# Linear attention with a highway layer: q in two-chunk pieces, weights loaded as f32, feed-forward in groups of two chunks, and another order in the fill

## The chip, the cores and the metric

The kernel runs on one core of a Trainium2 chip. A core has five engines that each run their own queue of instructions: TensorE (PE in the profile; its weight loads are PEld), VectorE (DVE), ScalarE (ACT), GpSimd (POOL) and SyncE (SP), which here only issues DMAs. Loads and stores run on 16 DMA engines. Matrix products are written to PSUM, which has eight banks; all else lies in SBUF. The metric is device time in microseconds, the median of ten runs. Lower is better.

## What is computed

Two stages follow one another. The first is a causal linear attention with a decay lam per head, over batch 4, 8 heads, 768 positions and head size 64:

```python
# in blocks; kv_state is 64 x 64 per batch and head
intra = (q_b @ k_b.T * Dmask) @ v_b          # Dmask[i, j] = lam**(i-j) for j <= i, else 0
inter = (q_b * lam_pow) @ kv_state
out_b = intra + inter
kv_state = lam_block * kv_state + (k_b * rev_pow).T @ v_b
```

The second takes the attention's output as x, 3072 tokens of 512 features, and applies a highway layer with two 512 x 512 weights:

```python
H = np.maximum(x @ w_h, 0.0)
T = 1.0 / (1.0 + np.exp(-(x @ w_t + b_t)))
out = T * H + (1.0 - T) * x
```

Inputs and output are f32. The kernel computes the products in bf16, and the last line as x + T * (max(x @ w_h, 0) - x).

## The kernel before

**Tiling.** Positions are cut in chunks of C = 128 tokens, six to a batch, so there are N = 24 chunks over the four batches. All 8 heads of a chunk are worked on together, as NP = 4 pairs of heads. The feed-forward takes G = 4 chunks at a time (512 tokens, GT), as four units, one for each 128 output features.

**Steps of a chunk n.** `cast_k` (L130) makes bf16 of k, and `scale_v` (L135) multiplies v by a power of lam and makes bf16 of it; both are on POOL. `trans_k` transposes k on PE with four transposes into the PSUM tile `tr`, and ACT copies that to `kT` (L166, L168). `scores` (L176) multiplies k by q with eight matmuls on half of the array, and DVE masks the result with a triangle (L179). `inter` (L187) applies the state `s_bd` to q, `intra` (L194) adds the masked scores times v into the same PSUM tile `o_ps`, and DVE scales that by `pow_q` into `xT` (L199). `state` (L208) adds the chunk to the state kept in PSUM, which ACT copies to `s_bd` in two halves (L212). The last chunk of a batch has no `state`, and the first has no `inter`.

**q.** Batch 0 is loaded chunk by chunk in rows of 256 bytes (`load_q0`, L67), cast by `cast_q0` and transposed by `trans_q0` (L146, L147). Batches 1 to 3 are loaded one pair of heads at a time with J = 6 tokens to a partition, in rows of 1536 bytes (`load_q`, L63), cast on POOL (L151), and transposed by `trans_q` in six transposes (L159) with one ACT copy that puts the tokens back in order (L160).

**Feed-forward.** `ffn_h` (L217) forms x @ w_h for one 128-feature slice in four matmuls of 512 columns, and DVE makes max(.,0) - x of it (L220). `ffn_t` (L225) does the same for w_t, with a sigmoid on ACT (L228) and a product on DVE (L231). `ffn_out` (L238) brings one chunk back to token order, adding x and the product with eight matmuls against the identity. ACT copies it to SBUF (L242; DVE for some of the last chunks, L244), and SP stores it (L245).

**PSUM.** Every tag has one buffer: `tr`, `s` (two banks), `o`, `kv`, `h`, `t` and `x` fill the eight banks. The next user of a tile waits for the reader of the last one.

**Order.** The order is written by hand: each engine runs its instructions in the order in which the program emits them. The loop's turn i emits the casts of chunk i+3, then `trans_k(i+2)`, `inter(i)`, `scores(i+1)`, `intra(i)`, `state(i)`, a q transpose, one feed-forward unit with one `ffn_out` between its two halves, and the loads of chunk i+8 (LA = 8). All loads of k, v and q are on SP's queue, and so are the stores. The two weights are loaded on POOL's queue with a cast to bf16 (L271, L272), after chunk 1's casts. The fill before the loop takes chunk 0 to its scores and chunk 1 to its transposes. Units of a group are queued when its last chunk is through `state`.

Of the kernel before, what the change touches and what calls it, by code (L numbers as in the profile page):

```python
# [16 lines left out]
def kernel(  # L17
# [43 lines left out]
    def load_q(b, hp):  # L61
        qf[b, hp] = load.tile([128, 2, J * D], F32, tag="qf", name="qf", bufs=6)
        nc.sync.dma_start(out=qf[b, hp], in_=q[b, 2 * hp:2 * hp + 2].rearrange("e (p j) d -> p e (j d)", j=J))  # L63

    def load_q0(c):
        q0f[c] = load.tile([C, H, D], F32, tag="q0f", name="q0f", bufs=4)
        nc.sync.dma_start(out=q0f[c], in_=q[0, :, c * C:(c + 1) * C, :].rearrange("h p d -> p h d"))  # L67

    def loads(n):
        if n >= N:  # L70
            return
        b, c = divmod(n, NCH)
        load_k(n)
        if b == 0:
            load_q0(c)
        load_v(n)
        if c < NP and b + 1 < B:
            load_q(b + 1, c)
# [40 lines left out]
    pow_q = singles.tile([128, NP, NCH * C], F32)  # L119
    for hp in range(NP):  # L120
        nc.scalar.activation(pow_q[:, hp, 0:C], tq_f[:, 0:C], AF.Exp, scale=ln_hp[:, hp:hp + 1])

    qb, kb, qT, kT, vs, masked, xT, thmx, hmx, kv_ps, o_ps = ({} for _ in range(11))

    def cast_k(n, eng=None):
        b, c = divmod(n, NCH)
        kb[n] = work.tile([C, H, D], BF16, tag="kb", name="kb", bufs=4)
        (eng or nc.gpsimd).tensor_copy(kb[n], kf[n])  # L130

    def scale_v(n):
        b, c = divmod(n, NCH)
        vs[n] = work.tile([C, H, D], BF16, tag="vs", name="vs", bufs=4)
        nc.gpsimd.tensor_tensor(vs[n], in0=vf[n], in1=pow_k[:, :, c, :].to_broadcast([C, H, D]), op=ALU.mult)  # L135

    def cast_q0(c, eng=None):
        qb[c] = work.tile([C, H, D], BF16, tag="q0b", name="q0b")
        (eng or nc.gpsimd).tensor_copy(qb[c], q0f[c])

    def trans_q0(c):
        if 0 not in qT:
            qT[0] = load.tile([128, NP, S], BF16, tag="qT", name="qT0")
        tr = ps.tile([128, NP, C], BF16, tag="tr", name="tr")
        for hp in range(NP):
            nc.tensor.transpose(tr[:, hp, :], qb[c][:, 2 * hp:2 * hp + 2, :], id128)  # L146
        nc.scalar.activation(qT[0][:, :, c * C:(c + 1) * C], tr, AF.Copy)  # L147

    def cast_q(b, hp):
        qb[b, hp] = work.tile([128, J, 2, D], BF16, tag="qb", name="qb")  # L150
        nc.gpsimd.tensor_copy(qb[b, hp].rearrange("p j e d -> p e j d"),  # L151
                              qf[b, hp].rearrange("p e (j d) -> p e j d", j=J))

    def trans_q(b, hp):
        if hp == 0:
            qT[b] = load.tile([128, NP, S], BF16, tag="qT", name=f"qT{b}")
        tr = ps.tile([128, J, 128], BF16, tag="tr", name="tr")
        for j in range(J):
            nc.tensor.transpose(tr[:, j, :], qb[b, hp][:, j], id128)  # L159
        nc.scalar.activation(qT[b][:, hp].rearrange("p (q j) -> p q j", j=J),  # L160
                             tr.rearrange("p j q -> p q j"), AF.Copy)
# [7 lines left out]

    def scores(n):  # L170
        b, c = divmod(n, NCH)
        s_ps = ps.tile([C, 2, NP, C], F32, tag="s", name="s_ps")
        for hp in range(NP):
            for e in range(2):
                r = slice(64 * e, 64 * e + 64)
                nc.tensor.matmul(s_ps[:, e, hp, :], lhsT=kT[n][r, hp, :], rhs=qT[b][r, hp, c * C:(c + 1) * C], start=True, stop=True)  # L176
# [4 lines left out]

    def inter(n):
        b, c = divmod(n, NCH)
        o_ps[n] = ps.tile([128, NP, C], F32, tag="o", name="o_ps")
        if c > 0:
            for hp in range(NP):
                nc.tensor.matmul(o_ps[n][:, hp, :], lhsT=s_bd[n % 2][:, hp, :], rhs=qT[b][:, hp, c * C:(c + 1) * C],  # L187
                                 start=(hp == 0), stop=False, skip_group_check=True)
# [25 lines left out]
    def ffn_h(g, j):  # L214
        h_ps = ps.tile([128, GT], F32, tag="h", name="h_ps")
        for kc in range(KC):
            nc.tensor.matmul(h_ps, lhsT=wh[:, kc, j * 128:(j + 1) * 128], rhs=xT[g][:, kc, :],  # L217
                             start=(kc == 0), stop=(kc == KC - 1))
        hmx[g, j] = work.tile([128, GT], BF16, tag="hmx", name="hmx")
        nc.vector.scalar_tensor_tensor(hmx[g, j], in0=h_ps, scalar=0.0, in1=xT[g][:, j, :], op0=ALU.max, op1=ALU.subtract)  # L220

    def ffn_t(g, j):
        t_ps = ps.tile([128, GT], F32, tag="t", name="t_ps")
        for kc in range(KC):
            nc.tensor.matmul(t_ps, lhsT=wt[:, kc, j * 128:(j + 1) * 128], rhs=xT[g][:, kc, :],  # L225
                             start=(kc == 0), stop=(kc == KC - 1))
        t_sb = work.tile([128, GT], BF16, tag="t_sb", name="t_sb")
        nc.scalar.activation(t_sb, t_ps, AF.Sigmoid, bias=bt_col[:, j:j + 1])  # L228
        if j == 0:
            thmx[g] = work.tile([128, NP, GT], BF16, tag="thmx", name="thmx")  # L230
        nc.vector.tensor_tensor(thmx[g][:, j, :], in0=t_sb, in1=hmx[g, j], op=ALU.mult)  # L231
# [19 lines left out]
    trans_k(0)
    trans_q0(0)
    scores(0)
    id_f = singles.tile([KC, KC], F32)
    nc.vector.tensor_copy(id_f, id128[0:KC, 0:KC])
    bt_ps = ps.tile([128, KC], F32, tag="x", name="bt_ps")
    nc.tensor.transpose(bt_ps, bt_r, id_f)
    bt_col = singles.tile([128, KC], F32)
    nc.vector.tensor_copy(bt_col, bt_ps)
    for n in range(4, LA):  # L260
# [1 line left out]
    cast_k(1)
    cast_q0(1)
    scale_v(1)
    trans_k(1)
    trans_q0(1)
    for hp in range(NP):
        nc.scalar.activation(pow_q[:, hp, C:], tq_f[:, C:], AF.Exp, scale=ln_hp[:, hp:hp + 1])
    wh = singles.tile([128, KC, DM], BF16)
    wt = singles.tile([128, KC, DM], BF16)  # L270
    nc.gpsimd.dma_start(out=wh, in_=moe_w_h.rearrange("(kc p) n -> p kc n", p=128))  # L271
    nc.gpsimd.dma_start(out=wt, in_=moe_w_t.rearrange("(kc p) n -> p kc n", p=128))  # L272
    cast_k(2)
    scale_v(2)
    cast_q0(2)
# [4 lines left out]
    while i < N or units or outs:  # L280
        b, c = divmod(i, NCH)
# [3 lines left out]
        if i + 3 < NCH:  # L285
            cast_q0(i + 3)
        if c < NP and b + 1 < B:
            cast_q(b + 1, c)
# [9 lines left out]
        if i + 2 < NCH:  # L298
            trans_q0(i + 2)
        if 1 <= c <= NP and b + 1 < B:  # L300
            trans_q(b + 1, c - 1)
        unit = units.pop(0) if units else None
        if unit:
            ffn_h(*unit)
        if outs:
            ffn_out(outs.pop(0), "dve" if i >= N and i % 2 else "act")
        if unit:
            ffn_t(*unit)
            if unit[1] == NP - 1:
                outs += range(unit[0] * G, unit[0] * G + G)  # L310
        if i < N and i % G == G - 1:
            units += [(i // G, j) for j in range(NP)]
# [32 lines left out]
```

## Time and profile before

| | |
|---|---|
| median of 10 runs | 138.34 us (137.11 to 139.17) |
| the profiled execution | 137.11 us, of which the span from the first to the last instruction is 135.2 us |
| PE busy | 101.4 us (75% of the span), 1105 instructions |
| DVE busy | 74.1 us (55%) |
| ACT busy | 77.6 us (57%) |
| POOL busy | 54.4 us (40%) |
| DMA | 26.40 MB in 64101 packets, of which 56916 are under 512 bytes |
| SP's and ACT's DMA packets | 77.9% of the 16 engines' span |
| the weights' packets (POOL's queue) | 4.7% |

Busy time is an average over stages that differ. In the slices of the profile each digit is the busy share of one fortieth of the span, in tenths. In the windows, the columns are the stretch in us, its length, then busy time and number of instructions of PE, PEld, DVE, ACT and POOL, then the granted TensorE clock as a share of full speed, the busy share of the DMA engines, and GB/s. A DMA share above 1 means that packets overlap. In the timeline, a line has its start, its length, the engine, the line of the kernel, the operation, what it writes and reads, and in brackets how long the engine had been idle and what ended that. Matmuls overlap in the array, so the length of a row of matmuls goes some 0.17 us beyond the start of the next.

### The profile page before, as it was taken

The page shows a single profiled execution, that of the slowest core. Times are in us where ns is not written, and L with a number is a line of the kernel's source. Part 1 is how long each engine was busy: PE and PEld are TensorE (multiplying, and loading weights), DVE is VectorE, ACT ScalarE, POOL GpSimd, SP SyncE. Part 2 cuts the span into 40 slices and gives each one's busy share as a digit, 9 for nine tenths or more (in the row PEclk, how much of TensorE's full clock was granted, in tenths as well). Part 3 has the DMA queues.
Part 4 walks back from the last instruction along what each step waited for, and adds up shares of the span by engine and source line. Part 5 has one row for each costly group of instructions (what it writes and reads, how often), then busy time and mean ns, then how long its engine had stood idle before and what let it go on. Part 6 is the DMA issues. An engine that isn't in the chain of part 4 may idle for free.

```text
span 135.2 us, 2889 instructions
## 1 busy us (share of the span) xinstructions
PE 101.4 (75%) x1105; PEld 67.1 (50%) x1121; DVE 74.1 (55%) x133; ACT 77.6 (57%) x141; POOL 54.4 (40%) x76
## 2 busy tenths in 40 slices
PE   0134520367674999999999999999999999999440
PEld 0122410345463655667766666766666665555330
DVE  4403230050432559976668878666887778656320
ACT  3752950144436665778885788887666766444310
POOL 5047620185596436767345776733243000000000
PEclk9999999999999599999999999999999999999975
DMA  2999999999999999999999999999222212224262
GB/s 62 257 245 266 235 191 213 231 233 225 184 257 268 259 266 192 219 266 215 229 265 273 260 253 256 267 276 263 87 82 78 78 62 81 94 78 158 82 228 78
DMA packets 64101, 26.40 MB, mean 195 GB/s; under 512 B 56916, under 2 KB 61016, under 8 KB 64088
## 3 DMA queue, kind: packets, MB, share of 16 engines
q1 hardware_dynamic: 62880, 25.17, 77.9%
q0 software_dynamic: 1056, 1.05, 4.7%
q8 instruction: 8, 0.13, 0.4%
q14 instruction: 5, 0.04, 0.1%
q10 hardware_dynamic: 152, 0.01, 0.1%
HBM read 20.98 MB, written 6.29 MB: 202 GB/s over the span
## 4 chain that ended last, share of the span: by engine, by line
PE 68%; SPq 9%; DMA 9%; ACT 6%; issue 3%; POOL 2%; DVE 1%; POOLq 0%; ACTq 0%
PE h_ps L217 16%; PE t_ps L225 15%; PE x_ps L238 9%; DMA kf<-in_k_dram 9%; PE o_ps L194 6%; PE s_ps L176 5%; PE kv_ps L208 5%; PE tr L159 4%; PE tr L166 4%; SPq L59 4%; PE o_ps L187 3%; SPq L63 3%; SPq L67 2%; ACT qT L160 2%; ACT qT L147 1%
## 5 line engine op out<-in xcount | busy, mean ns | idle before, releaser
L179 DVE TENSOR_TENSOR masked<-s_ps,tri 128x512 bf16<-128x512 f32 x48 | 30.8, 682 | 28.8 <-PE s_ps L176 28.8
L135 POOL TENSOR_TENSOR vs<-vf,pow_k 128x512 bf16<-128x512 f32 x24 | 25.4, 1059 | 22.3 <-DMA vf<-in_v_dram 11.0
L217 PE MATMUL h_ps<-xT,wh 128*128 128x512 bf16 x85 | 24.6, 389 | 0.7 <-issue 0.2
L225 PE MATMUL t_ps<-xT,wt 128*128 128x512 bf16 x91 | 24.4, 381 | 0.2
L130 POOL CAST kb<-kf 128x512 bf16<-128x512 f32 x23 | 14.1, 614 | 24.7 <-DMA kf<-in_k_dram 13.1
L166 PE MATMUL tr<-id,kb 128*128 128x128 bf16 x96 | 10.6, 240 | 16.7 <-POOL kb L130 8.9
L228 ACT ACTIVATE t_sb<-t_ps,bt_col 128x512 bf16<-128x512 f32 x24 | 16.5, 687 | 11.3 <-PE t_ps L225 9.8
L231 DVE TENSOR_TENSOR thmx<-t_sb,hmx 128x512 bf16<-128x512 bf16 x24 | 10.3, 429 | 20.0 <-ACT t_sb L228 19.7
L168 ACT ACTIVATE kT<-tr 128x512 bf16<-128x512 bf16 x24 | 14.2, 590 | 12.3 <-PE tr L166 12.3
L212 ACT ACTIVATE s_bd<-kv_ps 64x256 bf16<-64x256 f32 x40 | 15.1, 378 | 10.4 <-PE kv_ps L208 9.6
L166 PEld LDWEIGHTS <-kb 128*128 128x128 bf16 x96 | 7.8, 107 | 21.7 <-POOL kb L130 9.5
L242 ACT ACTIVATE o_sb<-x_ps 128x512 f32<-128x512 f32 x20 | 11.9, 597 | 11.2 <-PE x_ps L238 11.2
L220 DVE SCALAR_TENSOR_TENSOR hmx<-h_ps,xT 128x512 bf16<-128x512 f32 x24 | 16.3, 680 | 1.5 <-PE h_ps L217 1.5
L199 DVE TENSOR_TENSOR xT<-o_ps,pow_q 128x512 bf16<-128x512 f32 x24 | 16.3, 679 | 0.0
L238 PE MATMUL x_ps<-id,xT 128*128 128x128 bf16 x96 | 13.6, 222 | 2.6 <-ACT o_sb L242 1.4
L238 PE MATMUL x_ps<-id,thmx 128*128 128x128 bf16 x96 | 13.9, 223 | 0.4 <-DVE thmx L231 0.4
L238 PEld LDWEIGHTS <-thmx 128*128 128x128 bf16 x96 | 9.5, 99 | 6.2 <-issue 3.1
L217 PEld LDWEIGHTS <-wh 128*128 128x128 bf16 x96 | 8.6, 100 | 7.3 <-issue 0.6
L225 PEld LDWEIGHTS <-wt 128*128 128x128 bf16 x96 | 8.7, 99 | 7.0 <-issue 0.8
L160 ACT ACTIVATE qT<-tr 128x768 bf16<-128x768 bf16 x12 | 9.7, 811 | 2.6 <-PE tr L159 2.4
L176 PE MATMUL s_ps<-qT,kT 64*128 64x128 bf16 x192 | 10.6, 236 | 0.7 <-ACT qT L147 0.7
L194 PE MATMUL o_ps<-masked,vs 128*64 128x128 bf16 x192 | 10.9, 241 | 0.0
(45 smaller groups left out, 105.3 us busy)
## 6 DMA issues: line engine op xcount, KB each, us to landing
kf<-in_k_dram SPq DMA_DIRECT2D x24, 256.0 KB, 4.9
vf<-in_v_dram SPq DMA_DIRECT2D x24, 256.0 KB, 5.6
out_dram<-o_sb SPq DMA_DIRECT2D x24, 256.0 KB, 2.0
qf<-in_q_dram SPq DMA_DIRECT2D x12, 384.0 KB, 6.1
q0f<-in_q_dram SPq DMA_DIRECT2D x6, 256.0 KB, 5.7
wh<-in_moe_w_h_dram POOLq DMA_DIRECT2D x1, 512.0 KB, 8.8
wt<-in_moe_w_t_dram POOLq DMA_DIRECT2D x1, 512.0 KB, 11.2
lam_bc<-in_lam_dram ACTq DMA_DIRECT2D x1, 4.0 KB, 3.3
```

The source lines that it names most:

```text
L135: nc.gpsimd.tensor_tensor(vs[n], in0=vf[n], in1=pow_k[:, :, c, :].to_broadcast([C, H, D]), op=ALU.mult)
L166: nc.tensor.transpose(tr[:, hp, :], kb[n][:, 2 * hp:2 * hp + 2, :], id128)
L176: nc.tensor.matmul(s_ps[:, e, hp, :], lhsT=kT[n][r, hp, :], rhs=qT[b][r, hp, c * C:(c + 1) * C], start=True, stop=True)
L179: nc.vector.tensor_tensor(masked[n][:, e], in0=s_ps[:, e], in1=tri.to_broadcast([C, NP, C]), op=ALU.mult)
L194: nc.tensor.matmul(o_ps[n][64 * e:64 * e + 64, hp, :], lhsT=vs[n][:, 2 * hp + e, :], rhs=masked[n][:, e, hp, :], start=(hp == 0 and c == 0 ...
L199: nc.vector.tensor_tensor(xT[g][:, :, r * C:(r + 1) * C], in0=o_ps[n], in1=pow_q[:, :, c * C:(c + 1) * C], op=ALU.mult)
L212: nc.scalar.activation(s_bd[(n + 1) % 2][r, :, r], kv_ps[b][r, :, r], AF.Copy)
L217: nc.tensor.matmul(h_ps, lhsT=wh[:, kc, j * 128:(j + 1) * 128], rhs=xT[g][:, kc, :], start=(kc == 0), stop=(kc == KC - 1))
L220: nc.vector.scalar_tensor_tensor(hmx[g, j], in0=h_ps, scalar=0.0, in1=xT[g][:, j, :], op0=ALU.max, op1=ALU.subtract)
L225: nc.tensor.matmul(t_ps, lhsT=wt[:, kc, j * 128:(j + 1) * 128], rhs=xT[g][:, kc, :], start=(kc == 0), stop=(kc == KC - 1))
L228: nc.scalar.activation(t_sb, t_ps, AF.Sigmoid, bias=bt_col[:, j:j + 1])
L238: nc.tensor.matmul(x_ps[:, j * 128:(j + 1) * 128], lhsT=t[:, j, r * C:(r + 1) * C], rhs=id128, start=(j == 0 and i == 0), stop=(i == 1), s ...
```

## The change

q is loaded in pieces of two chunks for all batches, with two tokens to a partition, in rows of 512 bytes. One cast and one transpose step (eight transposes, one ACT copy of 1024 columns) serve two chunks. The separate path of batch 0 is gone.

The weights are loaded as f32 on SP's queue, in eight pieces, after the loads of chunks 0 and 1. Four casts on POOL and four on DVE make bf16 of them.

The feed-forward works on groups of two chunks (256 tokens), and of one chunk for the last two. A unit holds two 128-feature slices of a group of two, or all four of a group of one, so that a PSUM tile is full as before. Each slice has a sigmoid of its own, since each has its own bias.

In the fill, chunks 0 and 1 go all the way through attention, and the two units of their group run before the loop begins at i = 2. In the loop, `trans_k(i + 2)` stands at the end of turn i instead of ahead of `inter(i)`, and the q transposes stand at each even turn. LA is 10.

```diff
-    J = S // 128
+    J = 2
     N = B * NCH
-    G = 4
-    GT = G * C
-    LA = 8
+    LA = 10
+    sizes = [2] * (N // 2 - 1) + [1, 1]
+    first = [sum(sizes[:g]) for g in range(len(sizes))]
+    group = [g for g, z in enumerate(sizes) for _ in range(z)]
...
+    def load_q(s):
+        b, c = divmod(J * s, NCH)
+        qf[s] = load.tile([128, H, J * D], F32, tag="qf", name="qf", bufs=LA // J)
+        nc.sync.dma_start(out=qf[s], in_=q[b, :, c * C:(c + J) * C, :].rearrange("h (p j) d -> p h (j d)", j=J))
 
     def loads(n):
...
+        if n < N:
+            load_k(n)
+            if n % J == 0:
+                load_q(n // J)
+            load_v(n)
...
-    for n in range(4):
+    loads(0)
+    loads(1)
+    w_f, w_b = [], []
+    for w in (moe_w_h, moe_w_t):
+        w_f.append(singles.tile([128, KC, DM], F32, name=f"w_f{len(w_f)}"))
+        w_b.append(singles.tile([128, KC, DM], BF16, name=f"w_b{len(w_b)}"))
+        for kc in range(KC):
+            nc.sync.dma_start(out=w_f[-1][:, kc, :], in_=w[kc * 128:(kc + 1) * 128, :])
+    wh, wt = w_b
+    for n in range(2, LA):
         loads(n)
...
+    def cast_q(s, engs=None):
+        qb[s] = work.tile([128, J, H, D], BF16, tag="qb", name="qb")
+        engs = engs or [nc.gpsimd]
+        w = H // len(engs)
+        for i, eng in enumerate(engs):
+            h = slice(i * w, i * w + w)
+            eng.tensor_copy(qb[s].rearrange("p j h d -> p h j d")[:, h], qf[s].rearrange("p h (j d) -> p h j d", j=J)[:, h])
+
+    def trans_q(s):
+        tr = ps.tile([128, NP, J, 128], BF16, tag="tr", name="tr")
+        for hp in range(NP):
+            for j in range(J):
+                nc.tensor.transpose(tr[:, hp, j, :], qb[s][:, j, 2 * hp:2 * hp + 2, :], id128)
+        qT[s] = work.tile([128, NP, J * C], BF16, tag="qT", name="qT")
+        nc.scalar.activation(qT[s].rearrange("p n (q j) -> p n q j", j=J), tr.rearrange("p n j q -> p n q j"), AF.Copy)
...
+    def ffn_t(g, js, hmx):
+        T = sizes[g] * C
+        t_ps = ps.tile([128, len(js), T], F32, tag="t", name="t_ps")
+        for i, j in enumerate(js):
+            for kc in range(KC):
+                nc.tensor.matmul(t_ps[:, i, :], lhsT=wt[:, kc, j * 128:(j + 1) * 128], rhs=xT[g][:, kc, :],
+                                 start=(kc == 0), stop=(kc == KC - 1))
+        t_sb = work.tile([128, len(js), T], BF16, tag=f"t_sb{len(js)}", name="t_sb")
+        for i, j in enumerate(js):
+            nc.scalar.activation(t_sb[:, i, :], t_ps[:, i, :], AF.Sigmoid, bias=bt_col[:, j:j + 1])
...
+    def ffn_step(eng="act"):
+        unit = units.pop(0) if units else None
+        if unit:
+            hmx = ffn_h(*unit)
+        if outs:
+            ffn_out(outs.pop(0), eng)
+        if unit:
+            ffn_t(*unit, hmx)
+            g, js = unit
+            if js[-1] == NP - 1:
+                outs.extend(range(first[g], first[g] + sizes[g]))
+
+    def close(n):
+        if n == N - 1 or group[n + 1] != group[n]:
+            z = sizes[group[n]]
+            units.extend((group[n], list(range(j, j + NP // z))) for j in range(0, NP, NP // z))
...
     cast_k(0, nc.vector)
-    cast_q0(0, nc.vector)
+    cast_q(0, [nc.vector, nc.gpsimd])
+    trans_k(0)
+    trans_q(0)
+    scores(0)
     scale_v(0)
...
+    cast_k(1)
+    powers(0, 2 * C)
+    trans_k(1)
+    inter(0)
+    intra(0)
+    state(0)
+    scale_v(1)
+    scores(1)
+    for kc in range(KC):
+        (nc.vector if kc % 2 else nc.gpsimd).tensor_copy(wh[:, kc, :], w_f[0][:, kc, :])
+    powers(2 * C, S)
+    inter(1)
+    intra(1)
+    state(1)
+    for kc in range(KC):
+        (nc.vector if kc % 2 else nc.gpsimd).tensor_copy(wt[:, kc, :], w_f[1][:, kc, :])
+    close(1)
+    cast_k(2)
+    cast_q(1)
+    scale_v(2)
+    ffn_step()
+    ffn_step()
+    trans_k(2)
+    trans_q(1)
+    scores(2)
+    cast_k(3)
+    scale_v(3)
+    trans_k(3)
+    cast_k(4)
+    cast_q(2)
+    scale_v(4)
+
+
+    for n in range(LA, LA + 2):
         loads(n)
...
-    i = 0
+    i = 2
     while i < N or units or outs:
-        b, c = divmod(i, NCH)
         if i + 3 < N:
             cast_k(i + 3)
             scale_v(i + 3)
...
+            if i % J and (i + 3) % J == 0:
+                cast_q((i + 3) // J)
-        if i + 2 < N:
-            trans_k(i + 2)
         if i < N:
             inter(i)
         if i + 1 < N:
@@ -295,21 +331,13 @@
         if i < N:
             intra(i)
             state(i)
...
+        if i % J == 0 and i + 2 < N:
+            trans_q(i // J + 1)
+        ffn_step("dve" if i >= N and i % 2 else "act")
+        if i < N:
+            close(i)
+        if i + 2 < N:
+            trans_k(i + 2)
         loads(i + LA)
         i += 1
```

More of the change, by code (lines that the diff above doesn't have):

```diff
@@ L46 @@
     ps = ctx.enter_context(tc.tile_pool(name="ps", bufs=1, space=bass.MemoryType.PSUM))
-    kf, vf, qf, q0f = {}, {}, {}, {}
+    kf, vf, qf = {}, {}, {}
     def load_k(n):
@@ L59, in load_v @@
         nc.sync.dma_start(out=vf[n], in_=v[b, :, c * C:(c + 1) * C, :].rearrange("h p d -> p h d"))
[L61 to L67, printed above, removed]
-    def loads(n):
[L70 to L78, printed above, removed]
+    def load_q(s):
+        b, c = divmod(J * s, NCH)
+        qf[s] = load.tile([128, H, J * D], F32, tag="qf", name="qf", bufs=LA // J)
+        nc.sync.dma_start(out=qf[s], in_=q[b, :, c * C:(c + J) * C, :].rearrange("h (p j) d -> p h (j d)", j=J))
+    def loads(n):
+        if n < N:
[3 more added lines that the diff above has]
+            load_v(n)
     lam_bc = singles.tile([128, H], F32)
@@ L106 @@
     nc.vector.tensor_copy(tk_f, tk_i)
-    tq_f = singles.tile([128, NCH * C], F32)
+    tq_f = singles.tile([128, S], F32)
     nc.vector.tensor_copy(tq_f, tq_i)
@@ L118, with powers @@
     nc.scalar.activation(pow_k[:, :, :, 0], pk_ln, AF.Exp)
[L119 to L125, printed above, removed]
+    pow_q = singles.tile([128, NP, S], F32)
+    def powers(lo, hi):
+        for hp in range(NP):
+            nc.scalar.activation(pow_q[:, hp, lo:hi], tq_f[:, lo:hi], AF.Exp, scale=ln_hp[:, hp:hp + 1])
+    id_f = singles.tile([KC, KC], F32)
+    nc.vector.tensor_copy(id_f, id128[0:KC, 0:KC])
+    bt_ps = ps.tile([128, KC], F32, tag="x", name="bt_ps")
+    nc.tensor.transpose(bt_ps, bt_r, id_f)
+    bt_col = singles.tile([128, KC], F32)
+    nc.vector.tensor_copy(bt_col, bt_ps)
+    kb, qb, qT, kT, vs, masked, xT, thmx, kv_ps, o_ps = ({} for _ in range(10))
     def cast_k(n, eng=None):
-        b, c = divmod(n, NCH)
         kb[n] = work.tile([C, H, D], BF16, tag="kb", name="kb", bufs=4)
@@ L132, in scale_v @@
     def scale_v(n):
-        b, c = divmod(n, NCH)
+        c = n % NCH
         vs[n] = work.tile([C, H, D], BF16, tag="vs", name="vs", bufs=4)
         nc.gpsimd.tensor_tensor(vs[n], in0=vf[n], in1=pow_k[:, :, c, :].to_broadcast([C, H, D]), op=ALU.mult)
[L137 to L144, printed above, removed]
-        for hp in range(NP):
[L146 to L161, printed above, removed]
+    def cast_q(s, engs=None):
[7 more added lines that the diff above has]
+        tr = ps.tile([128, NP, J, 128], BF16, tag="tr", name="tr")
+        for hp in range(NP):
+            for j in range(J):
+                nc.tensor.transpose(tr[:, hp, j, :], qb[s][:, j, 2 * hp:2 * hp + 2, :], id128)
+        qT[s] = work.tile([128, NP, J * C], BF16, tag="qT", name="qT")
+        nc.scalar.activation(qT[s].rearrange("p n (q j) -> p n q j", j=J), tr.rearrange("p n j q -> p n q j"), AF.Copy)
     def trans_k(n):
@@ L168, in trans_k, with q_of @@
         nc.scalar.activation(kT[n], tr, AF.Copy)
+    def q_of(n, r, hp):
+        o = n % J * C
+        return qT[n // J][r, hp, o:o + C]
     def scores(n):
-        b, c = divmod(n, NCH)
         s_ps = ps.tile([C, 2, NP, C], F32, tag="s", name="s_ps")
@@ L175, in scores @@
                 r = slice(64 * e, 64 * e + 64)
-                nc.tensor.matmul(s_ps[:, e, hp, :], lhsT=kT[n][r, hp, :], rhs=qT[b][r, hp, c * C:(c + 1) * C], start=True, stop=True)
+                nc.tensor.matmul(s_ps[:, e, hp, :], lhsT=kT[n][r, hp, :], rhs=q_of(n, r, hp), start=True, stop=True)
         masked[n] = work.tile([C, 2, NP, C], BF16, tag="masked", name="masked")
@@ L182, in inter @@
     def inter(n):
-        b, c = divmod(n, NCH)
         o_ps[n] = ps.tile([128, NP, C], F32, tag="o", name="o_ps")
-        if c > 0:
+        if n % NCH:
             for hp in range(NP):
-                nc.tensor.matmul(o_ps[n][:, hp, :], lhsT=s_bd[n % 2][:, hp, :], rhs=qT[b][:, hp, c * C:(c + 1) * C],
+                nc.tensor.matmul(o_ps[n][:, hp, :], lhsT=s_bd[n % 2][:, hp, :], rhs=q_of(n, slice(0, 128), hp),
                                  start=(hp == 0), stop=False, skip_group_check=True)
     def intra(n):
-        b, c = divmod(n, NCH)
+        c = n % NCH
         for hp in range(NP):
@@ L195, in intra @@
                                  start=(hp == 0 and c == 0), stop=True, skip_group_check=True)
-        g, r = divmod(n, G)
+        g = group[n]
+        r = n - first[g]
         if r == 0:
-            xT[g] = work.tile([128, NP, GT], BF16, tag="xT", name="xT", bufs=3)
+            xT[g] = work.tile([128, NP, sizes[g] * C], BF16, tag=f"xT{sizes[g]}", name="xT", bufs=3)
         nc.vector.tensor_tensor(xT[g][:, :, r * C:(r + 1) * C], in0=o_ps[n], in1=pow_q[:, :, c * C:(c + 1) * C], op=ALU.mult)
@@ L212, in state @@
             nc.scalar.activation(s_bd[(n + 1) % 2][r, :, r], kv_ps[b][r, :, r], AF.Copy)
[L214 to L231, printed above, removed]
+    def ffn_h(g, js):
+        T = sizes[g] * C
+        h_ps = ps.tile([128, len(js), T], F32, tag="h", name="h_ps")
+        for i, j in enumerate(js):
+            for kc in range(KC):
+                nc.tensor.matmul(h_ps[:, i, :], lhsT=wh[:, kc, j * 128:(j + 1) * 128], rhs=xT[g][:, kc, :],
+                                 start=(kc == 0), stop=(kc == KC - 1))
+        hmx = work.tile([128, len(js), T], BF16, tag=f"hmx{len(js)}", name="hmx")
+        nc.vector.scalar_tensor_tensor(hmx, in0=h_ps, scalar=0.0, in1=xT[g][:, js[0]:js[-1] + 1, :],
+                                       op0=ALU.max, op1=ALU.subtract)
+        return hmx
@@ new lines, in ffn_t @@
+    def ffn_t(g, js, hmx):
+        T = sizes[g] * C
+        t_ps = ps.tile([128, len(js), T], F32, tag="t", name="t_ps")
+        for i, j in enumerate(js):
+            for kc in range(KC):
+                nc.tensor.matmul(t_ps[:, i, :], lhsT=wt[:, kc, j * 128:(j + 1) * 128], rhs=xT[g][:, kc, :],
+                                 start=(kc == 0), stop=(kc == KC - 1))
+        t_sb = work.tile([128, len(js), T], BF16, tag=f"t_sb{len(js)}", name="t_sb")
+        for i, j in enumerate(js):
+            nc.scalar.activation(t_sb[:, i, :], t_ps[:, i, :], AF.Sigmoid, bias=bt_col[:, j:j + 1])
+        if js[0] == 0:
+            thmx[g] = work.tile([128, NP, T], BF16, tag=f"thmx{sizes[g]}", name="thmx")
+        nc.vector.tensor_tensor(thmx[g][:, js[0]:js[-1] + 1, :], in0=t_sb, in1=hmx, op=ALU.mult)
@@ L233, in ffn_out @@
     def ffn_out(n, eng="act"):
-        g, r = divmod(n, G)
+        g = group[n]
+        r = n - first[g]
         x_ps = ps.tile([C, DM], F32, tag="x", name="x_ps")
@@ L245, in ffn_out @@
         nc.sync.dma_start(out=out[n * C:(n + 1) * C, :], in_=o_sb)
+    units, outs = [], []
+    def ffn_step(eng="act"):
[13 more added lines that the diff above has]
+            units.extend((group[n], list(range(j, j + NP // z))) for j in range(0, NP, NP // z))
@@ L248 @@
     cast_k(0, nc.vector)
-    cast_q0(0, nc.vector)
+    cast_q(0, [nc.vector, nc.gpsimd])
+    trans_k(0)
+    trans_q(0)
+    scores(0)
     scale_v(0)
[L251 to L260, printed above, removed]
-        loads(n)
@@ L262 @@
[L262 to L275, printed above, removed]
@@ L278 @@
-    units, outs = [], []
-    i = 0
+    cast_k(1)
[12 more added lines that the diff above has]
+    state(1)
+    for kc in range(KC):
+        (nc.vector if kc % 2 else nc.gpsimd).tensor_copy(wt[:, kc, :], w_f[1][:, kc, :])
+    close(1)
+    cast_k(2)
+    cast_q(1)
@@ L284 @@
             scale_v(i + 3)
[L285 to L288, printed above, removed]
-        if i + 2 < N:
-            trans_k(i + 2)
+            if i % J and (i + 3) % J == 0:
+                cast_q((i + 3) // J)
         if i < N:
@@ L297 @@
             state(i)
[L298 to L312, printed above, removed]
+        if i % J == 0 and i + 2 < N:
[5 more added lines that the diff above has]
+            trans_k(i + 2)
         loads(i + LA)
```

## Prediction

> **What bounds the kernel now.** I read the page's slices first, then the windows, the chain of waits, and the timeline of one turn of the loop ("turn i" is one pass, which emits scores(i+1) and intra(i)).
>
> ```profile
> PE   0134520367674999999999999999999999999440
> DMA  2999999999999999999999999999222212224262
> 20.00:25.00 5.00, 0.00 (x0) 0.00 (x0) 0.00 (x0) 0.00 (x0) 0.00 (x0) 1.00 1.23 222
> 40.00:50.00 10.00, 7.76 (x80) 5.23 (x82) 4.41 (x9) 6.79 (x11) 5.06 (x7) 0.83 1.15 262
> 70.00:80.00 10.00, 9.89 (x126) 6.64 (x127) 8.02 (x15) 7.05 (x14) 5.79 (x7) 1.00 1.12 274
> ```
>
> There are two stages. Up to about 46 us the loads set the pace: from 20 to 25 us no engine works at all while the DMA engines are full. After that TensorE is dense (9.9 of 10 us) until 125.3, and a tail of 9.9 us ends the span of 135.2.
>
> ```profile
> 13.56 11.53 DMA kf<-in_k_dram
> 25.14 0.61 POOL kb L130
> ```
>
> The chain shows the stall: k of chunk 3, issued at 13.56, lands 11.53 us later. Two things are in front of it or beside it: q pieces of batch 1 (384 KB each, not needed before chunk 6), and the cast loads of the weights, on POOL's queue from 12.60 on.
>
> ```profile
> 79.80 1.03 PE L225 MATMUL t_ps<-xT,wt 128*128 128x512 bf16 x4
> 80.00 0.60 ACT L242 ACTIVATE o_sb<-x_ps 128x512 f32<-128x512 f32 x1
> 80.66 0.39 PE L166 MATMUL tr<-id,kb 128*128 128x128 bf16 x4
> 80.86 0.69 ACT L228 ACTIVATE t_sb<-t_ps,bt_col 128x512 bf16<-128x512 f32 x1 [0.27 <-PE t_ps L225]
> 80.88 0.39 PE L187 MATMUL o_ps<-qT,s_bd 128*128 128x128 bf16 x4
> 81.20 0.40 PE L176 MATMUL s_ps<-qT,kT 64*128 64x128 bf16 x8
> 81.45 0.59 ACT L168 ACTIVATE kT<-tr 128x512 bf16<-128x512 bf16 x1
> ```
>
> The loop now: the k transposes (80.66) are followed by inter and scores without a gap. The copy to kT that they feed starts only at 81.45, after scores has begun: this kT is for the next turn. That distance of one turn is what keeps TensorE dense.
>
> **The fill, step by step.** Load prices come from waits that end on a landing.
>
> ```profile
> 5.79 0.43 DVE L139 CAST q0b<-q0f 128x512 bf16<-128x512 f32 x1 [0.78 <-DMA q0f<-in_q_dram]
> 6.94 1.06 POOL L135 TENSOR_TENSOR vs<-vf,pow_k 128x512 bf16<-128x512 f32 x1 [4.31 <-DMA vf<-in_v_dram]
> 9.37 0.61 POOL L130 CAST kb<-kf 128x512 bf16<-128x512 f32 x1 [1.37 <-DMA kf<-in_k_dram]
> ```
>
> A 256 KB load in 256 B rows takes 6.94 - 5.79 = 1.15 us (228 GB/s, 18 ns a row on each of 16 engines). Between 6.94 and 9.37 came such a load and one of 384 KB in 1536 B rows: 1.28 us for the latter (307 GB/s, 80 ns a row). No row of 512 B is shown for a load like the new q: between the ends, 18 ns and 80 ns, a straight line gives 30 ns, so 1.95 us for 512 KB; the ends are 2.3 us (the rate of 256 B rows) and 1.7 us (that of 1536 B rows). Weights in 2048 B rows: the packet records give 93 ns a store packet, so 0.75 us per 256 KB; at 307 GB/s it is 0.85.
>
> The Trainium skill ("DMA: Bandwidth & Descriptors", Specifications) says that line rate, 435 GB/s at the fabric, needs 512 B or more. By it 512 KB would take 1.2 us, and the four q pieces that count below would save 3 us. The 1536 B rows at 307 GB/s don't show that rate here, so I stay with 1.95.
>
> New order on SP: k0 lands 4.6, q0 6.5, v0 7.7, k1 8.8, v1 10.0, w_h 13.0, w_t 16.0, k2 17.1, q1 19.1, then 6.55 us per pair of chunks (1.95 + 4 x 1.15): k4 23.7, q2 25.6, k6 30.2, q3 32.2, v6 33.3. The eight weight casts (0.61 on POOL, 0.43 on DVE) lie under these landings; so do pow_q and the sigmoid table load (1.28). If that cover were gone, POOL's four would cost 2.4 us. On SP the weights stand in front of k2, which would land 6 us earlier without them; POOL is rid of 1.68 us of issuing them (12.60 to 14.28). id_f and bt_col (0.15 and 0.16 on DVE) move ahead of k0's landing, where DVE has nothing else. The group of chunks 0 and 1 runs its two feed-forward units between about 15 and 21 us, at the slow clock. POOL's order puts the cast of q3 behind scale_v(6): 33.3 + 1.06 + 1.04 (768 columns take 0.83, 512 take 0.61, so 1024 take 1.04) = 35.4. Turn 4's q transposes queue there, and all behind them on TensorE. My count of TensorE's own steps, in the cold durations of the fill (0.6 us for 4 transposes, 8 scores or 4 states) and with each wait on the one transpose buffer, gives: cast of q1 20.2, qT of chunks 2 and 3 ready 24.5, scores(2), kT3 25.8, scores(3) 25.9, turn 2's q transposes 26.8, their copy 29.1, trans_k(4) 29.7, kT4 30.4, scores(4) to the end of turn 3's store step 32.9, trans_k(5) 33.5, kT5 34.2, scores(5), intra, state 36.0. That is the same as the loads' 35.4 within what I can tell; I take 35.5. From there: 8 transposes 0.9, h 1.7 and t 1.7 at half speed, kT 1.25: scores(6) at 41.1. Before it is at 49.2. Bounds: 39.5 to 43.
>
> **The loop, per turn.** Now trans_k(i+2) stands at the end of turn i, and the next scores needs it: TensorE -> ScalarE -> TensorE in the open. Let T be the end of the last t matmul's stream (80.66 in the rows). ScalarE then does, in order: o_sb from T-0.67 to T-0.07; two sigmoids of 256 columns at 0.38 each (512 columns hold ScalarE 0.59, from 80.86 to 81.45; less 0.21 for 256 columns, the difference between the qT copies of 768 and 512 columns, 0.81 and 0.60; the s_bd copies of 256 columns hold it 0.39), to T+0.69; kT, then scores 0.65 after kT's start (as 29.61 to 30.26 in the fill): T+1.34. TensorE has only the transposes and inter to do, 0.44. Wait: 0.90 us in each turn. The low end is the chain without sigmoids in front: 0.20 latency after the transposes + 0.65, less inter: 0.63. The high end, both sigmoids only after the last t matmul: 1.16. I take 0.90. Queued behind it: intra and state, hence s_bd, the unit and the store.
>
> Other parts of a turn: feed-forward in 256 columns is 16 matmuls instead of 8; a straight line through 56 ns for 128 columns (x_ps) and 216 for 512 leaves 2.7 ns fixed for each: +0.02. ScalarE gets 0.17 more for the split sigmoid, 3.4 us of 4.75: not the bound. The q copies cost 12 x 1.03 instead of 6 x 0.61 + 12 x 0.81: nothing. DMA: 6.55 + 2 stores of 0.75 = 8.05 us a pair against 9.5 for TensorE, so loads lead once turn 5 runs, and a store that holds the loads on SP has ten chunks of cover; without it the loads would add some 1 us a turn.
>
> **Sum.** scores(6) to scores(23) takes 61.3 us before (49.20 to 110.52). After: + 0.9 (two more stores' x_ps at 0.45 fall in it) + 0.9 (8 x 2 more q transposes at 0.056) + 0.4 + 17 x 0.90 = 15.3: 78.8, to 119.9. From there to the last t: 14.8 before, less two units (3.5) and two x_ps (0.9): 10.4, to 130.3. Tail: 9.9 before, four chunks through x_ps and copy one after the other; after, one chunk: sigmoid 0.55, thmx 0.45, wait for x_ps 0.3, x_ps 0.6, copy 0.75, store 3.2: 5.8. Span 136.1 against 135.2. The profiled execution took 137.11 for its span, and is the fastest of ten runs with median 138.34; I carry the ratio over: 138.34 x 136.1 / 135.2 = 139.3 us. So 8 us won in the fill, 3.5 of units done early and 4 in the tail are given back by 15 of waits.
>
> **Rivals.** Each time is the span x 1.0232.
> 1. The wait is the bare chain, 0.63, since the sigmoids are over sooner than priced. For: ScalarE has 1.3 us a turn to spare. Against: its order, with o_sb and both sigmoids ahead of kT. 17 x 0.27 = 4.6 less: 131.5, 134.6 us, faster. It decides from 0.85 us a turn downward, where the span is that of before.
> 2. The clock falls. The windows show 0.83 at 40 to 50 us although TensorE was 7.76 busy: matmuls of half length at 42 (6 transposes in 0.49 where 0.80 stood before), doubled again at 45. A turn with 0.9 us idle and half-array matmuls could do the same. If one window in five of 3.4 us (the length in the clock records) is at half speed over 79 us, 4.6 x 1.7 = 7.8 us: 143.9, 147.2 us. Against: each such window holds over 70% work, while the one that led to the fall at 45 held some 40%.
> 3. The q rows cost what 256 B rows cost (the change doesn't do what it says): 4 x 0.35 = 1.4 us later at scores(6), 137.5, 140.7 us. Against: 1536 B rows are a third faster.
>
> On rival 2 the skill ("TensorE: Matmul & The Clock Gate", Part 1) says the clock falls after an idle window of about 3.4 us; by that the wait would cost no clock at all. The fall at 45 came after a window that was not idle, so the rule isn't enough here.
>
> **How the numbers follow.** Forecast 0.47 (own range 136.3 to 142.5), rival 1 0.25, rival 2 0.16, rival 3 0.12. A measurement of this kernel tells about 0.5% from no change. The forecast's share is split 0.07 faster, 0.12 same, 0.28 slower; with the rivals: faster 0.32, same 0.12, slower 0.56. The range, 133.0 to 146.5, reaches to rival 1 with an earlier fill and near rival 2.
>
> **What would show it.** scores(6) near 41; no 5 us of idle engines at 20; per turn 4.75 us from scores to scores, with "PE s_ps <- ACT kT" high among the waits (some 15 us); a tail under 6 us; the granted clock 1.0 from 45 on. I am wrong if turns stay at 3.9 us (some 124 us, the most that the edits could bring), or if the dense stage starts after 43.

## The result, and the profile after

The changed kernel takes 142.14 us (median of 11 runs, 141.25 to 143.82) against 138.08 before (38 runs): 1.036 times the time before, 95% interval 1.032 to 1.040. It is slower, and by more than the forecast's 0.7%. The ratio leaves out the slow runs of both kernels (over 1.5% above the fastest), so it is not the quotient of the two medians, 1.029. The profiled execution has a span of 139.9 us against 135.2.

The slices of the page after the change, and its windows with the columns as before:

```profile
PE   0257793789876977797779779778867977799950
DMA  1999999999987998999999999999522022102323
15.00:20.00 5.00, 4.44 (x33) 3.26 (x29) 3.01 (x5) 3.74 (x7) 1.83 (x4) 1.00 1.27 259
25.00:30.00 5.00, 3.92 (x44) 3.20 (x43) 3.15 (x5) 2.32 (x5) 3.15 (x4) 0.56 1.10 222
40.00:50.00 10.00, 7.27 (x104) 6.10 (x104) 7.01 (x11) 5.43 (x12) 4.86 (x6) 1.00 0.93 196
70.00:80.00 10.00, 7.83 (x114) 6.72 (x111) 6.32 (x12) 5.52 (x11) 3.67 (x4) 1.00 1.08 264
```

The stretch in which no engine worked is gone. TensorE works from 15 to 20 us, on the two units of chunks 0 and 1. But the row of nines that TensorE had from 50 us on is gone too: it is now busy for 7.8 of 10 us, until the last few turns. The granted clock is 1.00 from 40 to 130 us, so this is waiting and no throttle.

The list of waits of the changed kernel (total us, times, longest):

```profile
PE s_ps L179 <- ACT kT L168: 18.8, 20, 1.2
DVE thmx L242 <- ACT t_sb L239: 30.0, 24, 1.9
ACT s_bd L215 <- PE kv_ps L211: 25.2, 19, 2.3
```

Before, scores has no wait for kT in that list, which goes down to 0.2 us. The other two waits grew from 19.7 and 9.6 us. That of s_bd is a consequence of the first: with the first gone (first experiment below) it is 5.4. That of thmx stays at 24.2 there, so most of it is not. One turn in the timeline shows the place:

```profile
81.15 1.04 PE L235 MATMUL t_ps<-xT,w_b 128*128 128x256 bf16 x8
81.35 0.60 ACT L254 ACTIVATE o_sb<-x_ps 128x512 f32<-128x512 f32 x1 [0.54 <-PE x_ps L250]
82.02 0.39 PE L166 MATMUL tr<-id,kb 128*128 128x128 bf16 x4
82.22 0.84 ACT L239 ACTIVATE t_sb<-t_ps,bt_col 128x256 bf16<-128x256 f32 x2 [0.28 <-PE t_ps L235]
82.25 0.39 PE L189 MATMUL o_ps<-qT,s_bd 128*128 128x128 bf16 x4
82.95 0.60 ACT L168 ACTIVATE kT<-tr 128x512 bf16<-128x512 bf16 x1
83.61 0.40 PE L179 MATMUL s_ps<-qT,kT 64*128 64x128 bf16 x8 [0.97 <-ACT kT L168]
```

ScalarE is free at 81.95 but starts the first sigmoid only at 82.22, 0.20 after the last of the eight t matmuls, although the first slice's four, half of that row's work, were through some 0.44 earlier. Both sigmoids come after it (0.84 to their end), then kT, then scores. TensorE's stream of work ends at 82.47 with inter, and scores starts at 83.61: 1.14 us without new work, of which the profile's 0.97 leaves out the time that a matmul takes to drain. In the three turns whose chunk opens a batch there is no inter to cover the wait, and it is 1.36 (1.20 in the profile).

Where the span went, by the starts of scores in the timeline:

| | before | after | difference |
|---|---|---|---|
| to scores(6) | 49.14 | 40.56 | -8.6 |
| scores(6) to scores(23), 17 turns | 61.4 | 82.1 | +20.7 |
| scores(23) to the end | 24.7 | 17.3 | -7.4 |
| span | 135.2 | 139.9 | +4.7 |

The fill and the end gain 16 us, and the loop gives back 20.7.

### The profile page after: what moved, and what is told of

It is laid out like the page before. It is cut to its first block, busy times and chain, and to the rows that moved or that the text cites. A ratio compares the mean times of both kernels' runs of the same rounds, so it can differ in the third digit from the quotient of the medians.

```text
span 139.9 us, 3394 instructions
## 1 busy us (share of the span) xinstructions
PE 102.6 (73%) x1345; PEld 85.7 (61%) x1345; DVE 79.5 (57%) x135; ACT 81.2 (58%) x165; POOL 55.2 (39%) x73
## 4 chain that ended last, share of the span: by engine, by line
PE 49%; ACT 18%; SPq 16%; DMA 8%; issue 3%; DVE 2%; POOL 1%; POOLq 0%
PE t_ps L235 13%; PE h_ps L223 13%; ACT t_sb L239 12%; SPq L60 9%; PE x_ps L250 7%; ACT kT L168 6%; PE s_ps L179 5%; PE o_ps L196 5%; DMA vf<-in_v_dram 4%; SPq L55 4%; DMA w_f<-in_moe_w_h_dram 4%; PE kv_ps L211 4%; PE tr L159 3%; SPq L65 2%; SPq L85 1%
## 5 line engine op out<-in xcount | busy, mean ns | idle before, releaser
L145 POOL TENSOR_TENSOR vs<-vf,pow_k 128x512 bf16<-128x512 f32 x24 | 25.4, 1058 | 21.6 <-DMA vf<-in_v_dram 13.8
L242 DVE TENSOR_TENSOR thmx<-t_sb,hmx 128x512 bf16<-128x512 bf16 x24 | 12.7, 531 | 30.0 <-ACT t_sb L239 30.0
L239 ACT ACTIVATE t_sb<-t_ps,bt_col 128x256 bf16<-128x256 f32 (+1 forms) x52 | 20.8, 455 | 12.0 <-PE t_ps L235 12.0
L223 PE MATMUL h_ps<-xT,w_b 128*128 128x256 bf16 (+1 forms) x208 | 25.8, 270 | 0.6 <-DVE xT L202 0.6
L235 PE MATMUL t_ps<-xT,w_b 128*128 128x256 bf16 (+1 forms) x208 | 25.3, 267 | 0.1
L179 PEld LDWEIGHTS <-kT 64*128 64x128 bf16 x192 | 6.2, 101 | 26.1 <-ACT kT L168 23.5
L223 PEld LDWEIGHTS <-w_b 128*128 128x128 bf16 x208 | 18.5, 100 | 2.9 <-issue 0.7
L235 PEld LDWEIGHTS <-w_b 128*128 128x128 bf16 x208 | 18.6, 99 | 2.1 <-issue 0.2
L254 ACT ACTIVATE o_sb<-x_ps 128x512 f32<-128x512 f32 x22 | 13.1, 595 | 9.9 <-PE x_ps L250 9.8
L250 PE MATMUL x_ps<-id,xT 128*128 128x128 bf16 x96 | 14.2, 227 | 1.3 <-ACT o_sb L254 0.7
L153 POOL CAST qb<-qf 128x1024 bf16<-128x1024 f32 (+1 forms) x12 | 12.3, 1024 | 7.0 <-DMA qf<-in_q_dram 7.0
L161 ACT ACTIVATE qT<-tr 128x1024 bf16<-128x1024 bf16 x12 | 12.3, 1024 | 2.6 <-PE tr L159 2.3
```

Of the source, the lines that this page charges most:

```text
L223: nc.tensor.matmul(h_ps[:, i, :], lhsT=wh[:, kc, j * 128:(j + 1) * 128], rhs=xT[g][:, kc, :], start=(kc == 0), stop=(kc == KC - 1))
L235: nc.tensor.matmul(t_ps[:, i, :], lhsT=wt[:, kc, j * 128:(j + 1) * 128], rhs=xT[g][:, kc, :], start=(kc == 0), stop=(kc == KC - 1))
L239: nc.scalar.activation(t_sb[:, i, :], t_ps[:, i, :], AF.Sigmoid, bias=bt_col[:, j:j + 1])
L250: nc.tensor.matmul(x_ps[:, j * 128:(j + 1) * 128], lhsT=t[:, j, r * C:(r + 1) * C], rhs=id128, start=(j == 0 and i == 0), stop=(i == 1), s ...
```

## Experiments

Each was timed in three rounds against the kernel before, on the same chip (its medians there were 138.2 to 138.8). "Turn" is the time from one scores to the next, for even and odd turns; turns that nothing disturbs repeat to 0.02 us. Spans are of one profiled execution each, and executions of the changed kernel span 139.4 to 142.0 us, so a difference in span of a microsecond or two is told only where the turns show it.

**Undo the order of trans_k alone.** In the changed kernel:

```diff
+        if i + 2 < N:
+            trans_k(i + 2)
         if i < N:
             inter(i)
...
-        if i + 2 < N:
-            trans_k(i + 2)
         loads(i + LA)
```

> The changed kernel with trans_k(i+2) back ahead of inter(i), and nothing else undone. Theory W (kT's copy stands behind two sigmoids that both start after the last t matmul, and scores waits 1.14 us for it in every turn): scores to scores falls from 4.83 to some 3.7 us, 17 turns x 1.14 = 19.4 us off the span of 139.9, perhaps 1 more in the fill: 119 to 121, a median of some 122. Rival L (loads and stores set the pace of the dense stage, 8.05 us a pair of chunks): turns of 4.0 to 4.1 us, span 125 to 127, and waits on landings in place of kT. Rival F (matmuls of 256 columns, or the clock): turns stay above 4.5, span over 134.

Measured: 125.57 us, ratio 0.914 (0.902 to 0.927), span 123.2. Turns of 4.21 and 3.65 in place of 5.13 and 4.68: 0.92 and 1.03 a turn. scores(6) comes at 39.20, and the 17 turns take 66.7 us, 15.4 less than in the changed kernel. The timeline of one turn:

```profile
81.18 0.39 PE L166 MATMUL tr<-id,kb 128*128 128x128 bf16 x4
81.38 0.84 ACT L239 ACTIVATE t_sb<-t_ps,bt_col 128x256 bf16<-128x256 f32 x2 [0.15 <-PE t_ps L235]
81.41 0.39 PE L189 MATMUL o_ps<-qT,s_bd 128*128 128x128 bf16 x4
81.73 0.40 PE L179 MATMUL s_ps<-qT,kT 64*128 64x128 bf16 x8
82.11 0.60 ACT L168 ACTIVATE kT<-tr 128x512 bf16<-128x512 bf16 x1
```

ScalarE does the same work in the same order, with kT as late after the transposes as before (0.93, at 82.11), and scores does not wait for it: at 81.73 it uses the kT of the turn before. That settles the main question: one line's place made a faster kernel a slower one.

4.0 us of the 19.4 expected did not come. From inter to scores 0.32 goes by even here (81.41 to 81.73), 0.10 more than inter's 0.22 of work, so of the 1.14 only 1.04 was to be won. In even turns the q transposes come 0.36 after `state` where they came 0.23 after it, since kT's copy still holds the `tr` bank. And three turns, 4.93, 4.53 and 5.19, are longer than their like (4.21, 4.44, 4.21), 1.8 us in all. POOL waits longer for v (13.8 us in the changed kernel). In turn 20 q's cast is late behind v, and ScalarE waits for a store, so that kT and with it the q transposes come later still:

```profile
POOL vs L145 <- DMA vf<-in_v_dram: 26.9, 17, 3.8
97.46 0.60 ACT L254 ACTIVATE o_sb<-x_ps 128x512 f32<-128x512 f32 x1 [1.91 <-DMA out_dram<-o_sb]
99.32 0.61 PE L159 MATMUL tr<-id,qb 128*128 128x128 bf16 x8 [0.94 <-ACT kT L168]
```

**The same move, alone, in the kernel before.** trans_k(i+2) from the top of the turn to its end, and nothing else.

> The kernel before with trans_k(i+2) moved to the end of the turn, and nothing else of the change. W: one sigmoid of 512 columns (0.59) stands in front of kT, so the wait is 0.20 + 0.59 + 0.65 - 0.44 = 1.00 us a turn, in 17 turns: span 135.2 + 17 = 152, median some 155.5. L: the loads have slack in this kernel's dense stage, so it agrees with W or lies below. F (the wait is not what made the changed kernel slow): under 142.

Measured: 155.58 us, ratio 1.139 (1.128 to 1.150), span 153.8. Turns go from 3.96 and 3.62 to 4.85 and 4.51, 0.89 each. The timeline:

```profile
95.61 0.39 PE L166 MATMUL tr<-id,kb 128*128 128x128 bf16 x4
95.81 0.69 ACT L228 ACTIVATE t_sb<-t_ps,bt_col 128x512 bf16<-128x512 f32 x1 [0.27 <-PE t_ps L225]
96.40 0.59 ACT L168 ACTIVATE kT<-tr 128x512 bf16<-128x512 bf16 x1
97.04 0.40 PE L176 MATMUL s_ps<-qT,kT 64*128 64x128 bf16 x8 [0.82 <-ACT kT L168]
```

With one sigmoid of 512 columns in front, kT starts 0.79 after the transposes' start (95.61 to 96.40); with two of 256 it started 0.93 after it (82.02 to 82.95). The move has its price without any other part of the change. That the span came within 2 us of the forecast 152 is partly chance: the loop is 16.0 us longer, not 17, and scores(6) comes 2.6 later, which was not priced.

**trans_k between the store step and the t matmuls.** It was put into the unit, ahead of `ffn_t`, so that kT is copied ahead of the sigmoids.

> The changed kernel with trans_k(i+2) between the store step and the t matmuls of the unit, so that ScalarE copies kT ahead of the sigmoids. W: kT is ready 0.1 to 0.3 us after inter, turns of 3.8 to 4.0, span 121 to 124. L: 125 to 127 as with trans_k on top. F: over 134. If it is faster than trans_k on top, the sigmoids' lateness costs nothing and the earlier copy of q was in the way.

Measured: 127.22 us, ratio 0.928 (0.921 to 0.935), span 126.5, turns of 4.46 and 3.65. The span is 2.5 above the 121 to 124 expected. Odd turns are free of the wait. In even turns the transposes of k wait for ScalarE's copy of q's, which still holds the one `tr` bank:

```profile
PE tr L166 <- ACT qT L161: 2.0, 9, 0.3
```

**One sigmoid a unit.** The two activations of `ffn_t` became one of 512 columns, which leaves out the bias of every slice but the unit's first.

> The changed kernel with one sigmoid of 512 columns a unit in place of two of 256; b_t of the first slice stands for both, so the bias of the other slices is left out. It prices the split alone, at the same grouping. W (all that lies between the last t matmul and kT is paid by TensorE): 0.84 for two against some 0.68 for one up to kT's start, so 0.16 a turn, 17 turns: 2.7 us off the span of 139.9, 137.2. If the split is hidden: no change within 0.5 us.

Measured: 140.03 us, ratio 1.012 (1.004 to 1.021), span 138.5. Turns of 4.98 and 4.53, 0.15 less in both: the split alone costs 2.6 us over 17 turns, as expected. The span is 1.3 off the expected one because scores(6) came 1.7 later in this execution (42.28), after a turn that waited for loads.

**The first sigmoid between the two slices' matmuls.**

```diff
         for i, j in enumerate(js):
             for kc in range(KC):
                 nc.tensor.matmul(t_ps[:, i, :], ...)
-        for i, j in enumerate(js):
             nc.scalar.activation(t_sb[:, i, :], t_ps[:, i, :], AF.Sigmoid, ...)
```

> The changed kernel with the first slice's sigmoid emitted between the t matmuls of the two slices, which share a PSUM bank. If the first sigmoid could run beside the second slice's matmuls (as the prediction took it to), kT is copied 0.37 us earlier and the turn falls from 4.90 to some 4.55: span 134. If the reader and the writer of one bank take turns (then TensorE waits some 0.6 to 0.7 us in the middle, and the chain after the last t matmul is 0.36 shorter): turns of 5.1 to 5.3, span 143 to 146, with a wait of t_ps for t_sb in the list of waits.

Measured: 155.3 us, ratio 1.130 (1.121 to 1.140), span 153.6; turns of 5.55 and 5.09. The timeline:

```profile
81.67 0.60 PE L236 MATMUL t_ps<-xT,w_b 128*128 128x256 bf16 x4
82.37 0.48 ACT L238 ACTIVATE t_sb<-t_ps,bt_col 128x256 bf16<-128x256 f32 x1
82.90 0.60 PE L236 MATMUL t_ps<-xT,w_b 128*128 128x256 bf16 x4 [0.63 <-ACT t_sb L238]
```

The second slice's matmuls start 0.05 after the first sigmoid's end. So in this program the sigmoid does not run beside the matmuls that fill the other half of its bank: whichever is emitted first goes first. The two halves are also one tile, and no run put them in two tiles or two banks, so which of the two the order goes by is not told apart. The Trainium skill ("PSUM — Partial Sum Buffer", PSUM bank collisions raise a hardware error) states that two engines must not touch one bank and partition at a time, and that software has to see to it. The wait here agrees with such an order; that the chip would fail without it was not tried. The expected turns (5.1 to 5.3) hold on average over the 17, 5.24, but not the span: scores(6) was 2.3 later than in the changed kernel and the end, where a unit has four sigmoids, 4.3 longer. I had priced neither.

**Groups of four** after the first group of two: `sizes = [2] + [4] * 5 + [1, 1]`.

> The changed kernel with feed-forward groups of 2, five of 4, and 1, 1, so that nearly all h and t matmuls have 512 columns and one sigmoid each. W: the wait falls from 1.14 to 1.00 a turn, 17 x 0.14 = 2.4 us less: span 137 to 138. F: the columns were the cost, so span under 130. L: no change within 1 us.

Measured: 144.79 us, ratio 1.055 (1.040 to 1.070), span 143.9: a miss. The turns are shorter as expected, 4.97 and 4.51, and scores(23) comes 3.4 earlier, at 119.20. But from there to the end it takes 24.7 us instead of 17.3, as before the change. A group of four is not through until its last chunk is, so after scores(23) six units and ten output chunks are left in the trace, as many as before the change, instead of four and six. That is what the small groups earn: some 7 us at the end, for some 3 in the loop.

**The weights on POOL's queue**, cast while they are loaded as before the change, after scale_v(1).

> The changed kernel with the weights loaded on POOL's queue with a cast to bf16, as before the change, after scale_v(1); all else as changed. If the plain f32 loads in the load order earn part of the fill: the two units of chunks 0 and 1 wait for weights that land at 21 and 25 us, hold what stands behind them on TensorE, and scores(6) moves from 40.6 to 43 to 44: span 142 to 144. If the place of the weights is of no account: k of chunk 2 lands earlier, and the span stays at 139 to 140.5.

Measured: 145.56 us, ratio 1.058 (1.047 to 1.069), span 142.7; scores(6) at 43.34, turns unchanged. TensorE's timeline in the fill:

```profile
18.23 1.89 PE L220 MATMUL h_ps<-xT,w_b 128*128 128x256 bf16 x8 [2.52 <-DMA w_b<-in_moe_w_h_dram]
21.64 1.89 PE L232 MATMUL t_ps<-xT,w_b 128*128 128x256 bf16 x8 [1.52 <-DMA w_b<-in_moe_w_t_dram]
```

h starts at 18.23 where it had started at 16.38, t at 21.64 instead of 18.04. The two loads on SP's queue, as f32 and in their place in its order, earn 2.8 us together; how much of it is the queue, the cast while loading or the place is not told apart. That they earn something is clear of the noise, as the ratio's interval lies above the changed kernel's.

**No units in the fill.** The two calls of `ffn_step` ahead of the loop are gone.

> The changed kernel without the two feed-forward units in the fill; they run in the loop, and all later ones two turns later. If they lay in time that TensorE would have spent waiting for loads: scores(6) moves by less than 2 us against 40.6, and two more turns stand at the end, some 4 us: span 143 to 146. If they cost the fill as much as they save: 139 to 141.

Measured: 143.6 us, ratio 1.046 (1.034 to 1.057), span 142.5. scores(6) comes at 42.71, 2.1 later. The end takes 17.3 us as in the changed kernel: no two turns were added, because turns 2 and 3, which had no unit, took these. By the spans the units in the fill earn 2.6 us, not the 4 I had named, and by the medians 1.5. It is not clear of the noise: the ratio's interval overlaps with the changed kernel's (1.032 to 1.040), and in the run with one sigmoid scores(6) came 1.7 later although nothing in its fill was meant to delay it.

**With the wait away, what then?** Three kernels start from the one with trans_k on top (span 123.2). First, q in rows of 256 bytes.

> The changed kernel with trans_k on top (span 123.2), and q loaded in 256-byte rows, one DMA for each chunk of a piece. Packet records: 24576 x 20.5 ns against 12288 x 31.6 ns, 31.5 against 24.3 us of the 16 engines. If the loads pace this version (POOL waits 26.9 us for v), that is some 0.6 us a pair, 5 to 7 us over the span: 128 to 130. If TensorE paces it: 123 to 125.

Measured: 131.68 us, ratio 0.952 (0.946 to 0.959), span 129.9. The 512-byte rows are worth 6.7 us of span there, 3.4 of it before scores(6) and 3.3 in the 17 turns, so loads hold this version up in part. In packet records, one of 256 bytes took 20.8 ns and one of 512 bytes 31.6.

> The changed kernel with trans_k on top and, on POOL, the cast of q ahead of scale_v, since q lands before v. If the late turns of that version (4.93 and 5.19 us where 4.2 is usual) come from q's cast behind v: 1 to 2 us less, span 121.2 to 122.2. If they come from the landings themselves: no change, 123.

Measured: 126.85 us, ratio 0.912 (0.901 to 0.924), span 124.9. No change that can be told: the order of POOL's casts is not what makes the late turns. POOL's waits only move, for v from 26.9 to 9.6 us, for q from 7.8 to 19.6.

> The changed kernel with trans_k on top (span 123.2), and stores held back on SP until the last load is issued (12 buffers for the output). If loads and stores together pace that version, ten stores of some 0.7 us fewer stand among the loads, the turns fall to 4.2 and 3.65 throughout, and the span to 120 to 121.5. If not: 123, or more if the stores pile up at the end.

Measured: 133.28 us, ratio 0.971 (0.961 to 0.980), span 131.5. From turn 7 on all turns are 4.21 to 4.61 or 3.65 and less but one, of 11.78, in which ScalarE has no free buffer for an output chunk:

```profile
ACT o_sb L254 <- DMA out_dram<-o_sb: 9.3, 1, 9.3
```

SP issues the last load only at 88.77, as each issue before it takes 1.0 to 1.6 us from 79 us on, and the held stores begin behind it at 90.41; by then the twelve buffers are used up. With twenty:

> As with the stores held back, but 20 buffers for the output in place of 12, so that the thirteenth copy of an output chunk doesn't wait for a store. The turn of 11.8 us should be gone and all others stay at 4.2 and 3.65: scores(23) near 105, span 121.5 to 123. If the held stores delay the end (24 stores after 75 us): over 124.

Measured: 125.07 us, ratio 0.902 (0.893 to 0.911), span 123.4. The late turns are gone (4.21 and 3.65 to the end, 4.44 and 3.20 where a batch opens, scores(23) at 106.08), which fits the wait for a store in turn 20 of the run with trans_k on top. But two early ones, turns 4 and 6, are longer than with trans_k on top alone (5.33 and 5.51 against 5.04 and 4.93); why isn't settled. The interval overlaps with that of trans_k on top alone, so which of the two is the faster isn't settled. Both beat both kernels.

## Why the prediction was off

The direction held, and so did the mechanism: TensorE waits for a copy that stands behind the sigmoids. The term for it was too small. Step by step:

- **Fill: right, with some luck.** scores(6) was forecast at 41.1 and came at 40.56. The q transposes of turn 4, which the loads hold, came at 36.78 where 35.5 was taken. What follows took 3.8 us instead of 5.6, since the clock was back at full (0.91 on average from 35 to 40 us), where half speed had been taken. The two errors nearly cancel. The 512 KB pieces of q, priced at 1.95 us from a line between 256 and 1536 byte rows (30 ns a row), took 31.6 ns a row in the packet records. The weights were priced at 93 ns a packet; all packets of 2048 bytes, weights and stores, average 94.

```profile
36.78 0.62 PE L159 MATMUL tr<-id,qb 128*128 128x128 bf16 x8 [0.29 <-POOL qb L153]
37.23 1.04 PE L223 MATMUL h_ps<-xT,w_b 128*128 128x256 bf16 x8
```

- **The wait in the loop: right place, wrong size.** This is the step that failed. Of the three prices named (0.63, 0.90, 1.16) I took 0.90, in which the first sigmoid runs beside the second slice's matmuls. The measured wait is 1.14, at the upper bound: kT starts 0.93 after the last t matmul's stream, not 0.69. Of that, 0.10 lay between inter and scores before the change as well (80.88 to 81.20), so 14 turns grew by 1.04 and the three without an inter by 1.26: 18.3 us where the sum had 17 x 0.90 = 15.3. That is 3.0 of the 3.3 by which the loop came out over its 78.8. The end adds 1.1, the fill takes back 0.5, and the span is missed by 3.8. I treated the two sigmoids as two instructions with an input each. They read one tile in one bank, and both were emitted after the last matmul that writes it; the run with the sigmoid in between shows that the alternative is to hold TensorE instead.
- **The end:** forecast 10.4 + 5.8, measured 10.9 + 6.4. The tail's 0.6 is mainly the same mistake: the last unit's four sigmoids (1.14 us) all start after its last matmul, where I had put one behind it.
- **Units done early: about the right size, other cause.** The two units fewer at the end, priced at 3.5 us, are not those that ran in the fill. Without units in the fill the end has four units and takes 17.3 us all the same; with groups of four and the units still in the fill it has six and takes 24.7. The small groups earn this term as they earn the tail.
- **Loads off the path in the loop:** right for the changed kernel, whose turns repeat to 0.02 us from turn 6 on, with TensorE slowed by the wait. Without it single turns wait for landings or a store, and 256 byte rows of q cost 6.7 us. My 8.05 us a pair for loads and stores may have been somewhat high: most pairs of turns with trans_k on top take 7.86, though the loads' lead of ten chunks can hide a difference so small.
- **Rival 1** (a wait of 0.63) fell: kT starts 0.93 after the end of the t matmuls' stream, not 0.42. **Rival 2** (the clock): the clock did fall, to 0.56 and 0.50 between 25 and 35 us, in the fill, where the prediction had matmuls at half speed; in the loop it stayed at 1.00 with TensorE busy for 78% of the time. **Rival 3** (q rows as dear as 256 byte rows) fell by the packet records: 31.6 ns a row, where two rows of 256 bytes take 41.

## What to carry to other kernels

When an instruction that feeds another engine is moved, count how much work of its own engine lies between it and the first user of what comes back. One turn of distance hid a round trip of 1.6 us here; the new place left 0.44 of cover, and 17 turns of it, with the rest that the loop lost, outweighed the 16 us that the fill and the end had earned. When several reads are emitted behind several writes of one PSUM tile, price the reads as starting after the last write.

## What the runs showed of the hardware

- Longer rows were loaded faster: in the changed kernel's packet records a packet of 256 bytes took 20.5 ns, one of 512 bytes 31.6, and one of 2048 bytes (weights and stores) 94. On 16 engines, one packet after the other, that would be 200, 259 and 349 GB/s. Packets overlap in part (DMA shares up to 1.27), so these rates are on the low side.
- A sigmoid of 512 columns cut in two of 256 put 0.15 us more on the path of each turn.
- The clock fell between 25 and 30 us in the changed kernel (0.56 there, 1.00 before) after a stretch in which TensorE was busy for about half the time (2.64 of 5 us from 20 to 25), not idle; in the loop it stayed up with 78% (7.83 of 10 us from 70 to 80).
- The window from 15 to 20 us shows a clock of 1.00, but eight h matmuls that start at 16.38 take 1.86 us and eight that start at 19.28 take 1.04: the first ran at about half speed.
